# Pair-major order in 12 slots a pair, the MLP one batch behind, fp32 loads of batch 0, and deferred AV and output transposes

## The chip, the cores and the metric

The kernel runs on one core of a Trainium2 chip. The metric is the device time of one execution in microseconds. Each kernel was run several times. The kernel before takes 350.33 us (median of 4 runs, 350.21 to 351.83).

## The reference

Attention with a choice of key chunks, then a two-layer MLP with a softplus. There are 4 batches, 8 heads, 768 positions and 64 values a head; the MLP is 512 to 2048 to 512.

```python
k_min, k_max = k chunk-wise (24 chunks of 32 keys)
ub  = sum_d max(q*k_min, q*k_max)          # upper bound of each query for each chunk
top = the 6 best causal chunks of each query
p   = softmax(scale * q @ k.T, only the chosen chunks, causal)
x   = (p @ v) as [3072 tokens, 512]
out = softplus(x @ w_in) @ w_out           # float32
```

All inputs are float32 in memory; the kernel computes in bf16.

## The kernel before

Two heads make a pair: 4 pairs a batch, 16 in all. A pair is prepared (transposes of k and q, chunk maxima and minima, bound, choice of chunks, a mask row added to the score operands) and then has three blocks of 256 queries with 2, 4 and 6 score steps. A score step is two matmuls of up to 256 columns and one exp on ScalarE. An MLP block is 256 tokens; it needs the same block of all four pairs of its batch. It is cut into 8 `h` pieces (8 matmuls of 256 columns and an exp; after every second piece a log) and 8 `y` pieces (4 matmuls of 512 columns).

```python
def load(i):                                # all loads cast fp32 -> bf16 in flight, from GpSimd
    for h in range(2):
        nc.gpsimd.dma_start(out=k_sb[:, :, h, :], in_=k[b, 2*p+h]...)
        nc.gpsimd.dma_start(out=q_sb[:, :, h, :], in_=q[b, 2*p+h]...)
# ... load(0..2), load_v(0..2), then w_in (4 loads); w_out in the preparation of pair 1

steps = [(b*NP + p, blk) for b in range(B) for blk in range(NBLK) for p in range(NP)]  # block-major
for s_idx, st in enumerate(steps):
    # score_step(st); av_step of the step before; ot_step of the one before that;
    # preparation up to 6 steps ahead; the MLP paced by pump() at RATIO = 1.75
```

Each score step's diagonal block is masked by an `affine_select` on GpSimd; `av_step` multiplies by v into `o_ps` and divides into `o_sb`; `ot_step` transposes into `xT`, which the MLP reads. The framework's scheduler sets the order of the instructions on each engine; the order of the Python program is its input and is not always what stands in the queues.

The softmax here doesn't subtract the row's maximum and nothing guards it: scores larger than these inputs give would overflow.

## Time and profile before

| | before |
|---|---|
| median time | 350.33 us |
| TensorE busy | 281.8 us, 80% |
| first score exp | 28.7 us |
| first exp of the MLP ("MLP start") | 78.2 us |
| last score exp ends | 318.0 us |
| span minus MLP start | 272.3 us |

First, the page of the kernel before: busy time, the busy tenths in 40 slices of 8.76 us, and the chain that ended last.

```profile
PE 281.8 (80%) x2784; PEld 202.2 (58%) x2784; DVE 171.5 (49%) x580; ACT 218.1 (62%) x369; POOL 140.1 (40%) x274
...
PE   1003254389889989999999899999999999999994
...
POOL 8994877961682744350514443101112211000000
...
DMA  9999999990795864443703444000000000000111
...
PE 49%; POOL 16%; ACT 15%; DMA 7%; issue 7%; DVE 4%; POOLq 0%; ACTq 0%; DVEq 0%
```

TensorE (PE) is at most half busy in the first eight slices, in which GpSimd (POOL) is mostly full and the DMA engines are full; from slice nine on TensorE is nearly full. So an average of 80% hides two stages. The next view cuts the span at the MLP start and at the last score exp. Its columns are the busy time (and instructions) of PE, PEld, DVE, ACT and POOL, then the granted clock, the DMA share and GB/s.

```profile
0.00:78.20 78.20, 26.63 (x221) 19.32 (x222) 46.03 (x156) 16.47 (x27) 63.62 (x105) 1.00 1.43 124
78.20:318.00 239.80, 228.12 (x2387) 166.70 (x2386) 120.83 (x415) 188.70 (x326) 76.06 (x168) 1.00 0.32 39
318.00:350.50 32.50, 27.10 (x180) 16.16 (x177) 4.64 (x9) 12.95 (x18) 0.41 (x1) 0.98 0.11 41
```

TensorE works 26.6 of the first 78.2 us. By the timeline, only 15 of the 192 score exps are done by then. In the shared stretch it is busy 95%, but a busy TensorE is not one at its peak. The starts of its instructions give the better measure: an MLP piece takes 0.87 us, and a pair's whole attention about 5.3 us, 0.44 us a score step. Counted in the trace, with the cost of each kind of matmul that the prediction below lists, the shared stretch holds 177 score steps (192 - 15), about 161 MLP pieces and the preparations, AV products and transposes that fall into it: 214 us of work in 239.8 us. Part of the rest is in the list of waits of the kernel before from 78 us on (engine and line, whom it waited for: us in total, times, longest):

```profile
PEld L244 <- POOL pt L229: 10.4, 21, 1.2
PE o_ps L244 <- POOL pt L229: 6.6, 14, 1.1
```

The AV products (L244) wait for the diagonal select on GpSimd (L229). The two lines overlap, since PEld is the weight load of the same matmuls.

### The profile page before, as it was taken

The numbers are of one execution on the slowest core, as the hardware profiler recorded it, in microseconds if no ns is written. First come the engines' busy times: TensorE is split into PE (matmuls) and PEld (weight loads), VectorE is DVE, ScalarE is ACT, GpSimd is POOL, SyncE is SP. The second block draws the span as 40 slices with busy tenths as digits, with TensorE's granted clock in tenths as the row PEclk, the third lists the DMA queues.
The fourth block names the chain that finished last, engine by engine and source line by source line (L and its number), as shares of the span: only waits on it lengthen the run. The fifth ranks groups of instructions, "written<-read, shape, count | busy, mean of one in ns | idle before, by whom it ended". The sixth has DMA issues, their size and how long they took to land.

```text
span 350.5 us, 7076 instructions
## 1 busy us (share of the span) xinstructions
PE 281.8 (80%) x2784; PEld 202.2 (58%) x2784; DVE 171.5 (49%) x580; ACT 218.1 (62%) x369; POOL 140.1 (40%) x274
## 2 busy tenths in 40 slices
PE   1003254389889989999999899999999999999994
PEld 1002133268567656766776567767767777766651
DVE  3875285644773645674726456647165321212101
ACT  1102022259879749677987596879876878876640
POOL 8994877961682744350514443101112211000000
PEclk9999999999999999999999999999999999999999
DMA  9999999990795864443703444000000000000111
GB/s 67 80 145 189 136 192 129 109 66 1 49 86 37 77 46 54 52 30 49 75 33 36 41 55 52 2 32 32 30 32 4 33 30 32 30 2 32 46 46 60
DMA packets 81441, 20.38 MB, mean 58 GB/s; under 512 B 75776, under 2 KB 77824, under 8 KB 81408
## 3 DMA queue, kind: packets, MB, share of 16 engines
q0 software_dynamic: 77952, 13.64, 49.7%
q1 hardware_dynamic: 3456, 6.29, 4.8%
q8 instruction: 22, 0.36, 0.4%
q14 instruction: 11, 0.09, 0.1%
HBM read 27.26 MB, written 6.29 MB: 96 GB/s over the span
## 4 chain that ended last, share of the span: by engine, by line
PE 49%; POOL 16%; ACT 15%; DMA 7%; issue 7%; DVE 4%; POOLq 0%; ACTq 0%; DVEq 0%
PE hp L282 18%; PE y L297 15%; ACT pt L225 6%; PE o_ps L244 5%; ACT e_sb L284 4%; DMA w_out_sb<-in_moe_w_out_dram 4%; POOL k_sb L77 4%; PE s_ps L220 4%; POOL q_sb L79 4%; ACT g L286 3%; DMA w_in_sb<-in_moe_w_in_dram 3%; POOL pt L229 3%; PE s_ps L223 2%; PE mT L202 2%; PE kT L142 1%
## 5 line engine op out<-in xcount | busy, mean ns | idle before, releaser
L225 ACT ACTIVATE pt<-s_ps 128x512 bf16<-128x512 f32 (+1 forms) x192 | 99.6, 544 | 69.3 <-PE s_ps L223 68.2
L297 PE MATMUL y<-w_out_sb,g 128*128 128x512 bf16 x384 | 100.4, 379 | 1.6 <-DVE y_sb L302 1.6
L229 POOL TENSOR_SCALAR_AFFINE_SELECT pt<-pt 128x256 bf16<-128x256 bf16 x96 | 38.8, 409 | 127.2 <-ACT pt L225 126.1
L284 ACT ACTIVATE e_sb<-hp 128x512 f32<-128x512 f32 x96 | 57.0, 597 | 37.3 <-PE hp L282 36.5
L282 PEld LDWEIGHTS <-w_in_sb 128*128 128x128 bf16 x768 | 72.4, 99 | 13.4 <-issue 1.2
L282 PE MATMUL hp<-xT_221,w_in_sb 128*128 128x256 bf16 x192 | 53.1, 277 | 0.0
L282 PE MATMUL hp<-xT_222,w_in_sb 128*128 128x256 bf16 x192 | 52.7, 276 | 0.0
L282 PE MATMUL hp<-xT_223,w_in_sb 128*128 128x256 bf16 x192 | 52.3, 275 | 0.0
L282 PE MATMUL hp<-xT_224,w_in_sb 128*128 128x256 bf16 x192 | 51.6, 275 | 0.4
L286 ACT ACTIVATE g<-e_sb 128x1024 bf16<-128x1024 f32 x48 | 50.8, 1059 | 0.5
L244 PEld LDWEIGHTS <-pt 128*128 128x128 bf16 x672 | 33.5, 99 | 27.9 <-POOL pt L229 20.0
L297 PEld LDWEIGHTS <-g 128*128 128x128 bf16 x384 | 34.5, 97 | 25.6 <-issue 2.1
L249 DVE RECIPROCAL rec<-o_ps 128x4 f32<-128x4 f32 x48 | 8.5, 178 | 67.4 <-PE o_ps L244 67.4
L77 POOL DMA_DIRECT2D k_sb<-in_k_dram x32 | 27.3, 855 | 25.5 <-PE kT L142 21.3
L79 POOL DMA_DIRECT2D q_sb<-in_q_dram x32 | 27.3, 854 | 5.4 <-PE qT L156 3.5
L302 DVE COPY y_sb<-y 128x512 f32<-128x512 f32 x24 | 16.4, 684 | 26.3 <-PE y L297 26.3
L185 DVE TENSOR_TENSOR ub_sb<-ub,cmask 128x288 f32<-128x288 f32 x16 | 7.3, 454 | 27.3 <-PE ub L183 27.2
L251 DVE TENSOR_TENSOR o_sb<-o_ps,rec 128x256 bf16<-128x256 f32 x48 | 20.1, 418 | 1.1
L182 PEld LDWEIGHTS <-qpos 128*128 128x128 bf16 x96 | 7.3, 101 | 22.7 <-DVE qpos L171 17.0
L203 DVE COPY qa<-mT 32x768 bf16<-32x768 bf16 x16 | 8.8, 548 | 19.7 <-PE mT L202 19.7
L145 DVE TENSOR_REDUCE kx<-kT 128x24 bf16<-128x768 bf16 x16 | 15.2, 952 | 4.2 <-PE kT L142 4.0
L182 PE MATMUL ub<-bd_0_151,qpos 128*128 128x48 bf16 x48 | 4.4, 191 | 15.4 <-POOL bd_0_151 L151 14.2
(237 smaller groups left out, 461.7 us busy)
## 6 DMA issues: line engine op xcount, KB each, us to landing
out_dram<-y_sb SPq DMA_DIRECT2D x24, 256.0 KB, 2.0
k_sb<-in_k_dram POOLq DMA_DIRECT2D x32, 96.0 KB, 3.3
q_sb<-in_q_dram POOLq DMA_DIRECT2D x32, 96.0 KB, 3.5
w_in_sb<-in_moe_w_in_dram POOLq DMA_DIRECT2D x4, 512.0 KB, 8.9
w_out_sb<-in_moe_w_out_dram POOLq DMA_DIRECT2D x4, 512.0 KB, 10.3
v_98<-in_v_dram POOLq DMA_DIRECT2D x4, 96.0 KB, 3.8
v_99<-in_v_dram POOLq DMA_DIRECT2D x4, 96.0 KB, 3.3
v_100<-in_v_dram POOLq DMA_DIRECT2D x4, 96.0 KB, 3.5
```

Of the source, the lines that this page charges most:

```text
L77: nc.gpsimd.dma_start(out=k_sb[:, :, h, :], in_=k[b, 2 * p + h].rearrange("(t s) d -> s t d", s=128))
L79: nc.gpsimd.dma_start(out=q_sb[:, :, h, :], in_=q[b, 2 * p + h].rearrange("(t s) d -> s t d", s=128))
L145: nc.vector.tensor_reduce(kx[:, 0], kT3, axis=AX.X, op=ALU.max)
L225: nc.scalar.activation(pt[:, h, j:j + 2].rearrange("k j c -> k (j c)")[:, 0:n], s_ps[:, 0:n], ACT.Exp, scale=scale)
L229: nc.gpsimd.affine_select(out=diag, in_=diag, compare_op=ALU.is_ge, fill=0.0, base=0, channel_multiplier=-1, pattern=[[0, 2], [1, 128]])
L244: nc.tensor.matmul(o_ps[:, u, h], pt[:, h, j, c0:c0 + 128], v_sb[i % NV][:, j, h, :], start=(j == 0), stop=(j == t0 + u))
L251: nc.vector.tensor_tensor(o_sb, o_ps[:, :, :, 0:D], rec.to_broadcast([128, 2, 2, D]), op=ALU.mult)
L282: nc.tensor.matmul(hp[:, fi], w_in_sb[:, dt, ft * 128:(ft + 1) * 128], xT[dt][:, cs], start=(dt == 0), stop=(dt == KDM - 1))
L284: nc.scalar.activation(e_sb[:, f2 * 2:f2 * 2 + 2], hp, ACT.Exp)
L286: nc.scalar.activation(g[:, f4 * 4:(f4 + 1) * 4], e_sb, ACT.Ln, bias=1.0)
L297: nc.tensor.matmul(y, g[:, f, u * 128:(u + 1) * 128], w_out_sb[:, f, :], start=(f == 0), stop=(f == KFF - 1))
L302: nc.vector.tensor_copy(y_sb, y)
```

## The change

Its intent is to fill the idle start with attention work and to let TensorE wait less.

- Order: pair-major. A pair has 12 slots of one score step each; a slot also takes one deferred piece and one MLP piece, and slots 0, 1, 4 and 8 a piece of the next pair's preparation. The MLP runs about one batch behind. With the order came fewer buffers (k 8 to 4, v 12 to 5, q 8 to 4), one more for the MLP's `g`, and loads two pairs ahead instead of three.
- Loads: q and k of batch 0 come as fp32 from the SP queue (SyncE's DMA queue, HWDGE in the skill's terms) and are cast on ScalarE. The Trainium skill, "DMA: Bandwidth & Descriptors", section "SWDGE vs HWDGE vs iDMA", says that only GpSimd's DMAs can cast in flight; hence the fp32 buffers. For batch 0 some small copies also move from GpSimd to VectorE and from VectorE to ScalarE.
- Deferral: an AV product is due two slots after its scores, an output transpose two slots after its AV.

```diff
+    def load_f32(i):
+        for nm, x in (("k", k), ("q", q)):
+            xf = f_pool.tile([128, NQT, 2, D], F32, name="xf")      # 4 buffers
+            for h in range(2):
+                nc.sync.dma_start(out=xf[:, :, h, :], in_=x[b, 2 * p + h]...)
+            nc.scalar.copy(xb, xf)
-    load(1); load_v(1); load(2); load_v(2)
+    load_f32(1); load_v(1)
     for kt in range(KDM):                      # w_in: place unchanged
         nc.gpsimd.dma_start(out=w_in_sb[:, kt, :], in_=moe_w_in[...])
@@ prep_pair(i)
+        n = i + 2
+        load_f32(n) if n < NP else load_cast(n);  load_v(n)
@@ the order
+        later.append((clock[0] + 2, av_step(i, blk, pt)))        # and ot_step in the same way
+    PREP_AT = (0, 1, 4, 8)
+    for i in range(len(pairs)):
+        for blk in range(NBLK):
+            for _ in score_step(i, blk):
+                slot([nxt] if idx in PREP_AT else [])   # prep piece, one due piece, one MLP piece
...
```

More of the change, by code (lines that the diff above doesn't have):

```diff
@@ L1 @@
 import math
+from collections import deque
 from contextlib import ExitStack
@@ L43 @@
     NBLK = S // QB
-    NK = 8
-    NV = 12
+    NK = 4
+    NV = 5
     nc.scalar.preload_act_table_set("natural_log_exp_and_others")
+    PS = bass.MemoryType.PSUM
     singles = ctx.enter_context(tc.tile_pool(name="singles", bufs=1))
+    f_pool = ctx.enter_context(tc.tile_pool(name="f", bufs=4))
     io_pool = ctx.enter_context(tc.tile_pool(name="io", bufs=3))
-    qt_pool = ctx.enter_context(tc.tile_pool(name="qt", bufs=8))
+    qt_pool = ctx.enter_context(tc.tile_pool(name="qt", bufs=4))
     prep = ctx.enter_context(tc.tile_pool(name="prep", bufs=2))
@@ L54 @@
     st_pool = ctx.enter_context(tc.tile_pool(name="st", bufs=3))
-    g_pool = ctx.enter_context(tc.tile_pool(name="g", bufs=2))
+    g_pool = ctx.enter_context(tc.tile_pool(name="g", bufs=3))
     e_pool = ctx.enter_context(tc.tile_pool(name="e", bufs=3))
     mo_pool = ctx.enter_context(tc.tile_pool(name="mo", bufs=3))
-    PS = bass.MemoryType.PSUM
     ps_s = ctx.enter_context(tc.tile_pool(name="ps_s", bufs=2, space=PS))
@@ L67, with load_cast @@
     KB = [singles.tile([128, S], BF16, name=f"kb_{i}") for i in range(NK)]
+    w_in_sb = singles.tile([128, KDM, d_ff], BF16, name="w_in_sb")
+    w_out_sb = singles.tile([128, KFF, d_model], BF16, name="w_out_sb")
+    xT = [singles.tile([128, NTOK], BF16, name=f"xT_{p}") for p in range(NP)]
     pairs = [(b, p) for b in range(B) for p in range(NP)]
     loaded = {}
-    def load(i):
-        b, p = pairs[i]
-        q_sb = io_pool.tile([128, NQT, 2, D], BF16, name="q_sb")
-        k_sb = io_pool.tile([128, NQT, 2, D], BF16, name="k_sb")
-        for h in range(2):
-            nc.gpsimd.dma_start(out=k_sb[:, :, h, :],
-                                in_=k[b, 2 * p + h].rearrange("(t s) d -> s t d", s=128))
-            nc.gpsimd.dma_start(out=q_sb[:, :, h, :],
-                                in_=q[b, 2 * p + h].rearrange("(t s) d -> s t d", s=128))
-        loaded[i] = (q_sb, k_sb)
+    def load_f32(i):
+        for nm, x in (("k", k), ("q", q)):
+            xf = f_pool.tile([128, NQT, 2, D], F32, name="xf")
+            b, p = pairs[i]
+            for h in range(2):
+                nc.sync.dma_start(out=xf[:, :, h, :],
+                                  in_=x[b, 2 * p + h].rearrange("(t s) d -> s t d", s=128))
+            xb = io_pool.tile([128, NQT, 2, D], BF16, name=nm + "_sb")
+            nc.scalar.copy(xb, xf)
+            loaded[nm, i] = xb
+    def load_cast(i):
+        for nm, x in (("k", k), ("q", q)):
+            xb = io_pool.tile([128, NQT, 2, D], BF16, name=nm + "_sb")
+            b, p = pairs[i]
+            for h in range(2):
+                nc.gpsimd.dma_start(out=xb[:, :, h, :],
+                                    in_=x[b, 2 * p + h].rearrange("(t s) d -> s t d", s=128))
+            loaded[nm, i] = xb
     def load_v(i):
@@ L87, in load_v @@
                                 in_=v[b, 2 * p + h].rearrange("(t s) d -> s t d", s=128))
-    load(0)
-    load_v(0)
     ident = singles.tile([128, 128], BF16)
     make_identity(nc, ident)
+    load_f32(0)
+    load_v(0)
     cmask = singles.tile([128, NQT, NCH], F32, name="cmask")
@@ L114, with init_k @@
         nc.vector.memset(v_sb[i][:, :, :, D:D + 1], 1.0)
-    for i in range(NK):
+    def init_k(i):
         nc.vector.tensor_copy(KA[i][64:96, :], ohb)
@@ L118 @@
         nc.vector.tensor_copy(KB[i][32:64, :], ohb)
-    w_in_sb = singles.tile([128, KDM, d_ff], BF16, name="w_in_sb")
-    w_out_sb = singles.tile([128, KFF, d_model], BF16, name="w_out_sb")
-    load(1)
+    load_f32(1)
     load_v(1)
-    load(2)
-    load_v(2)
     for kt in range(KDM):
         nc.gpsimd.dma_start(out=w_in_sb[:, kt, :], in_=moe_w_in[kt * 128:(kt + 1) * 128, :])
-    xT = [singles.tile([128, NTOK], BF16, name=f"xT_{p}") for p in range(NP)]
-    QA = {}
-    QT = {}
+    QA, QT, owner = {}, {}, {}
     def prep_pair(i):
-        q_sb, k_sb = loaded.pop(i)
         ka, kb = KA[i % NK], KB[i % NK]
@@ L138, in prep_pair @@
         mraw = Mraw[i % 2]
+        early = i < NP
+        if i < NK:
+            init_k(i)
+        k_sb = loaded.pop(("k", i))
+        q_sb = loaded.pop(("q", i))
         kT = ps_t.tile([128, S], BF16, name="kT", tag="t")
@@ L148, in prep_pair @@
         nc.scalar.copy(kb[64:128, :], kT[64:128, :])
+        eng = nc.vector if early else nc.gpsimd
         for m, dst in enumerate((kmx, kmn)):
             for h in range(2):
-                nc.gpsimd.tensor_copy(dst[h * 64:(h + 1) * 64, h], kx[h * 64:(h + 1) * 64, m])
-        yield 0.35
+                eng.tensor_copy(dst[h * 64:(h + 1) * 64, h], kx[h * 64:(h + 1) * 64, m])
+        owner["k", i % NK] = i
+        yield
         qT = ps_t.tile([128, S], BF16, name="qT", tag="t")
@@ L156, in prep_pair @@
             nc.tensor.transpose(qT[:, t * 128:(t + 1) * 128], q_sb[:, t], ident)
-        if i + 3 < len(pairs):
-            load(i + 3)
-            load_v(i + 3)
+        n = i + 2
+        if n < len(pairs):
+            if n < NP:
+                load_f32(n)
+            else:
+                load_cast(n)
+            load_v(n)
+            owner["v", n % NV] = n
         if i == 1:
@@ L169, in prep_pair @@
         qneg = prep.tile([128, S], BF16, name="qneg")
-        nc.vector.tensor_copy(qt, qT)
+        if early:
+            nc.scalar.copy(qt, qT)
+        else:
+            nc.vector.tensor_copy(qt, qT)
         nc.vector.tensor_scalar_max(qpos, qt, 0.0)
@@ L174, in prep_pair @@
         QA[i], QT[i] = qa, qt
-        yield 0.35
-        yield 0.0
-        yield 0.0
+        yield
         ub = ps_t.tile([128, NQT, 2, NCH], F32, name="ub", tag="t")
@@ L194, in prep_pair @@
         nc.vector.tensor_copy(mraw[:, :, :, NCH:NCH + 1], m8[:, :, :, 0:1])
-        yield 0.35
-        yield 0.0
-        yield 0.0
-        yield 0.0
+        yield
         mT = ps_t.tile([64, S], BF16, name="mT", tag="t")
@@ L204, in prep_pair, with score_step @@
         nc.vector.tensor_copy(qt[32:64, :], mT[32:64, :])
-        yield 0.3
-    PT = {}
-    def score_step(st):
-        i, blk = st
+        yield
+    later = deque()
+    done = {}
+    clock = [0]
+    def score_step(i, blk):
+        assert owner["k", i % NK] == i
         t0 = 2 * blk
         pt = pt_pool.tile([128, 2, NQT, QB], BF16, name="pt")
-        PT[st] = pt
         for h in range(2):
@@ L226, in score_step, with av_step @@
                                      s_ps[:, 0:n], ACT.Exp, scale=scale)
-                yield 0.25
-            diag = pt[:, h, t0:t0 + 2, 0:128]
-            nc.gpsimd.affine_select(out=diag, in_=diag, compare_op=ALU.is_ge, fill=0.0,
-                                    base=0, channel_multiplier=-1,
-                                    pattern=[[0, 2], [1, 128]])
-    OS = {}
-    def av_step(st):
-        i, blk = st
+                if last:
+                    diag = pt[:, h, t0:t0 + 2, 0:128]
+                    nc.gpsimd.affine_select(out=diag, in_=diag, compare_op=ALU.is_ge, fill=0.0,
+                                            base=0, channel_multiplier=-1,
+                                            pattern=[[0, 2], [1, 128]])
+                yield
+        later.append((clock[0] + 2, av_step(i, blk, pt)))
+    def av_step(i, blk, pt):
         t0 = 2 * blk
-        pt = PT.pop(st)
         o_ps = ps_o.tile([128, 2, 2, D + 1], F32, name="o_ps")
@@ L246, in av_step @@
                                      start=(j == 0), stop=(j == t0 + u))
-            yield 0.1 * (t0 + u + 1)
+            if u == 0:
+                yield
         rec = st_pool.tile([128, 2, 2, 1], F32, name="rec")
@@ L252, in av_step, with ot_step @@
                                 rec.to_broadcast([128, 2, 2, D]), op=ALU.mult)
-        OS[st] = o_sb
-    def ot_step(st):
-        i, blk = st
+        later.append((clock[0] + 2, ot_step(i, blk, o_sb)))
+        yield
+    def ot_step(i, blk, o_sb):
         b, p = pairs[i]
-        o_sb = OS.pop(st)
         oT = ps_t.tile([128, QB], BF16, name="oT", tag="t")
@@ L264, in ot_step @@
         done[(b, blk)] = done.get((b, blk), 0) + 1
-        yield 0.12
-    done = {}
+        yield
     mlp_blocks = [(b, blk) for b in range(B) for blk in range(NBLK)]
+    G = {}
     def h_gen(n):
@@ L286, in h_gen @@
                     nc.scalar.activation(g[:, f4 * 4:(f4 + 1) * 4], e_sb, ACT.Ln, bias=1.0)
-                yield 0.87
-    G = {}
+                yield
     def y_gen(n):
@@ L304, in y_gen @@
                         nc.sync.dma_start(out=out[r0:r0 + 128, :], in_=y_sb)
-                    yield 0.87
+                    yield
     def mlp_stream():
@@ L309, in mlp_stream @@
         for n in range(len(mlp_blocks) + 1):
+            hg = iter(())
             if n < len(mlp_blocks):
                 while done.get(mlp_blocks[n], 0) < NP:
-                    yield None
+                    yield "wait"
                 hg = h_gen(n)
-            else:
-                hg = iter(())
             yg = y_gen(prev) if prev is not None else iter(())
-            for a in hg:
-                yield a
-                c = next(yg, None)
-                if c is not None:
-                    yield c
@@ L322, in mlp_stream @@
-            for c in yg:
-                yield c
+            for _ in hg:
+                yield
+                if next(yg, "end") != "end":
+                    yield
+            for _ in yg:
+                yield
             prev = n
     mlp = mlp_stream()
-    state = dict(attn=0.0, mlp=0.0)
-    ATT_TOTAL = 100.0
-    MLP_TOTAL = 167.0
-    RATIO = 1.75
-    LAG = 0.0
-    AHEAD = 6
-    def pump(cost):
-        state["attn"] += cost
-        while state["mlp"] < state["attn"] * RATIO - LAG:
-            c = next(mlp, "end")
-            if c is None or c == "end":
-                if c is None:
-                    state["mlp"] = max(state["mlp"], state["attn"] * RATIO - LAG - 2.0)
-                return
-            state["mlp"] += c
@@ L344, in chain @@
-    def chain(*gens):
-        for g_ in gens:
-            yield from g_
-    steps = []
-    for b in range(B):
-        for blk in range(NBLK):
-            for p in range(NP):
-                steps.append((b * NP + p, blk))
-    def drain(g_):
-        for c in g_:
-            pump(c)
-    side_done = []
-    def side_stream():
-        for i in range(len(pairs)):
-            yield from prep_pair(i)
-            side_done.append(i)
-    side = side_stream()
-    order = steps
-    for s_idx, st in enumerate(order):
-        while len(side_done) <= st[0]:
-            s = next(side, None)
-            if s is not None:
-                pump(s)
-        tail_gens = []
-        if s_idx >= 1:
-            tail_gens.append(av_step(order[s_idx - 1]))
-        if s_idx >= 2:
-            tail_gens.append(ot_step(order[s_idx - 2]))
-        tail = chain(*tail_gens)
-        ahead = order[min(s_idx + AHEAD, len(order) - 1)][0]
-        for c in score_step(st):
-            pump(c)
-            t_ = next(tail, None)
-            if t_ is not None:
-                pump(t_)
-            if len(side_done) <= min(ahead + 1, len(pairs) - 1):
-                s = next(side, None)
-                if s is not None:
-                    pump(s)
-        for t_ in tail:
-            pump(t_)
@@ L390, with slot @@
-    drain(av_step(order[-1]))
-    drain(ot_step(order[-2]))
-    drain(ot_step(order[-1]))
-    for c in mlp:
+    def slot(piece_gens=()):
+        for g_ in piece_gens:
+            next(g_, None)
+        if later and later[0][0] <= clock[0]:
+            g_ = later[0][1]
+            if next(g_, "end") == "end":
+                later.popleft()
+                if later and later[0][0] <= clock[0]:
+                    next(later[0][1], None)
+        next(mlp, None)
+        clock[0] += 1
@@ L394 @@
+    PREP_AT = (0, 1, 4, 8)
+    for _ in prep_pair(0):
+        pass
+    for i in range(len(pairs)):
+        nxt = prep_pair(i + 1) if i + 1 < len(pairs) else iter(())
+        idx = 0
+        for blk in range(NBLK):
+            for _ in score_step(i, blk):
+                slot([nxt] if idx in PREP_AT else [])
+                idx += 1
+        for _ in nxt:
+            pass
+    while later:
+        slot()
+    for _ in mlp:
         pass
```

## The prediction

> **What bounds the kernel now.** TensorE is busy 80% of the 350.5 us (page, part 1), but unevenly. The 40 slices and the table by window show two regimes. From 0 to about 77 us TensorE is busy under 40%; the last chain of waits there runs through GpSimd issuing casting loads (k_sb and q_sb, about 0.85 us each) and through waits for the w_in and w_out DMAs (11.9 and 13.2 us pieces). From about 80 us on TensorE is 90-100% busy and the chain is hp and y matmuls. The MLP's first pieces stand at about 77 us in the chain; it then needs 270 us.
>
> **Costs read from the timeline (start to start).** One MLP piece takes 0.87 us (8 hp matmuls at 0.109, or 4 y matmuls at 0.215). Per pair: kT and qT 0.34 each, ub 0.30, mT 0.46, scores 2.3, AV 42 x 0.03 = 1.26, oT 3 x 0.11: about 5.3 us, 0.44 per score slot. Sum: 192 x 0.87 + 16 x 5.3 = 252 us that TensorE must spend. A slot plus a piece is 1.31 us of TensorE work; before needs about 1.42 (windows 140 to 260: about 84 slots and 85 pieces). ScalarE needs about 1.05 us per such slot, so TensorE stays the bound there.
>
> **What changes.** Nothing leaves TensorE. (1) Pair-major order needs all four pairs of a batch nearly finished before its MLP starts: by the slot rules at slot 43; it pauses at slots 83 to 91, and some 50 pieces are left after the last slot (50 x 0.87 = 43 us, TensorE alone, well packed). (2) Before 77 us the kernel now does 43 attention slots, against about 10 before: that fills the idle start. (3) Batch 0's q and k leave the casting queue: GpSimd issues 2 loads a pair instead of 6 (saves about 3.4 us a pair) and no longer copies bd early. The Trainium skill, "DMA: Bandwidth & Descriptors", section on SWDGE vs HWDGE, says that a cast in flight is possible only from GpSimd, hence the fp32 buffers and ScalarE casts (estimate 0.8 us each from the 0.79 us copies). The same page says that all issuers share 16 DMA engines, so bytes and 256-byte descriptors still queue there; the trace has no such HWDGE load to show their rate. (4) AV and oT deferred two slots: removes most TensorE waits for the diagonal select (about 20 us of waits over the span, about 10 in the first 80 us).
>
> **Sum.** First slot: ScalarE's in-order queue makes pair 0's qt copy wait for casts of pairs 1 and 2, which compete with w_in: landing about 20-22 us, plus a 6 us selection chain: 28 us. Attention-only slots are bound by VectorE (about 10.6 us of work a pair) and ScalarE (about 9): 43 slots at 0.95 = 41 us, MLP start at 69 us. Then 141 shared slots at 1.36 = 192, 8 slots alone 7, 51 pieces 44, last y copy and store 3. Total 315 us.
>
> **Prediction: 315 us, range 299 to 337.** Faster by over 2%: 0.91; within 2%: 0.07; slower by over 2%: 0.02.
>
> **What the profile would show.** First score exp at 22-34 us; first hp matmul at 60-78 us; in the shared stretch 16.3 us per pair with TensorE over 95% busy; a pure MLP tail of 38-46 us; waits of o_ps for the select nearly gone; ScalarE waits for DMA xf in the first 25 us.
>
> **What would make it wrong.** HWDGE loads with 256-byte descriptors far slower than 0.8 descriptors per ns (seen for GpSimd's loads), or starved by w_in: each pair's delay adds directly before the MLP start. Shared slots no better than 1.42: +8 us. Attention-only slots chain-bound at 1.2 us: +11 us.

## The result, and the profile after

The changed kernel takes 322.9 us (median of 4 runs, 322.04 to 323.86). The ratio to the kernel before is 0.9209 (95% interval 0.9173 to 0.9245).

The page after, same lines without DMA:

```profile
PE 278.0 (86%) x2784; PEld 203.4 (63%) x2784; DVE 167.9 (52%) x573; ACT 225.0 (70%) x381; POOL 123.9 (38%) x242
...
PE   1213788698999999899999999999999999999984
...
POOL 8401688846444545558191919131212111000000
...
PE 78%; ACT 7%; SPq 4%; DMA 4%; DVE 3%; issue 2%; POOL 1%; ACTq 0%; POOLq 0%
```

The chain is now 78% TensorE instead of 49%, with GpSimd down from 16% to 1%. The stretches of the kernel after, cut at the same events:

```profile
0.00:79.80 79.80, 44.26 (x421) 32.08 (x422) 48.15 (x182) 41.77 (x71) 45.18 (x77) 0.89 1.15 132
79.80:270.50 190.70, 188.32 (x2055) 142.74 (x2055) 113.44 (x380) 158.56 (x279) 78.36 (x164) 1.00 0.46 48
270.50:322.00 51.50, 45.41 (x311) 28.61 (x309) 6.34 (x11) 24.65 (x33) 0.41 (x1) 0.99 0.11 42
```

This is the main reading. The MLP does not start earlier: 79.8 us against 78.2. But by then 47 score exps are done instead of 15, and what follows takes 242.2 us (322.0 - 79.8) instead of 272.3. Counted in the two traces as above, the TensorE work before the MLP start is 22.9 us after and 12.3 before, so about 10.6 us moved into the start. (The 32 steps at 0.44 would make 14, but the 0.44 includes the preparation, which was about equally far in both kernels: the k and q of five pairs were transposed.) The shared stretch now holds 145 score steps and about 140 pieces, 185 us of work in 190.7, so about 6 us are lost where before lost about 26. The sum, 10.6 + 20, is about the 30 us that the part after the MLP start became shorter. The select's waits after 80 us are nearly gone:

```profile
PEld L260 <- POOL pt L247: 0.3, 1, 0.3
PEld L277 <- DVE o_sb L268: 0.3, 1, 0.3
```

(L260 is the AV product and L277 the output transpose of the kernel after.)

Why does the MLP not start earlier, with fewer loads on GpSimd? The timeline of the SP queue after (start, us, what):

```profile
0.81 1.01 SPq L82 DMA_DIRECT2D xf<-in_k_dram  x2
1.88 1.21 SPq L82 DMA_DIRECT2D xf<-in_q_dram  x2
3.13 2.92 SPq L82 DMA_DIRECT2D xf<-in_k_dram  x2
6.10 2.35 SPq L82 DMA_DIRECT2D xf<-in_q_dram  x2
8.57 11.29 SPq L82 DMA_DIRECT2D xf<-in_k_dram  x2
```

and of ScalarE, with GpSimd's w_in line between:

```profile
7.80 2.18 POOL L138 DMA_DIRECT2D w_in_sb<-in_moe_w_in_dram  x4
...
24.19 0.83 ACT L85 CAST q_sb<-xf 128x768 bf16<-128x768 f32 x1 [10.23 <-DMA xf<-in_q_dram]
25.05 0.79 ACT L160 COPY kb_110<-kT 64x768 bf16<-64x768 bf16 x1
...
29.37 0.83 ACT L85 CAST q_sb<-xf 128x768 bf16<-128x768 f32 x1 [0.85 <-DMA xf<-in_q_dram]
30.23 0.87 ACT L243 ACTIVATE pt<-s_ps 128x384 bf16<-128x384 f32 x2
```

Pair 1's q was issued at 6.1 us. w_in was issued from 7.8 us on, and the q landed only at 24.2 us; the SP queue's next two issues took 11.29 us (2.83 us for the same two in e7 below, where no weight is in flight). ScalarE works in order: pair 0's last k copy (25.05) stood behind the cast of pair 1's q, and the first score exp, whose matmul began at 26.5 us, stood behind the cast of pair 2's q (29.37) and came at 30.2 us.

The packets that the packed trace records show the crowding itself. From 12 to 20 us, beside w_in, the SP queue's packets of 256 bytes start at 53 per us, about one for each of w_in's 48 packets of 4096 bytes per us. From 27 to 31 us, alone, they start at 822 per us.

A second thing stands in the timeline of TensorE in the attention-only stretch of the kernel after:

```profile
39.04 0.42 PE L238 MATMUL s_ps<-qa,ka_106 96*128 96x256 bf16 x1
39.26 0.31 PE L241 MATMUL s_ps<-qa,ka_106 96*128 96x128 bf16 x1
...
92.83 0.27 PE L238 MATMUL s_ps<-qa,ka_106 96*128 96x256 bf16 x1
92.94 0.27 PE L241 MATMUL s_ps<-qa,ka_106 96*128 96x256 bf16 x1
```

The matmul of 256 columns keeps TensorE 0.22 us at 39 us and 0.11 us at 92 us. The Trainium skill, "TensorE: Matmul & The Clock Gate", Part 1, says that the array runs at half its clock by default and that sustained activity releases it; the factor of two agrees. The page's clock column shows 1.00 at 39 us all the same, because it has no record before 48.4 us (in the kernel before, none before 79.6 us, so the 1.00 of its first stretch is no measurement either). Between 64 and 72 us it records 0.50.

### The profile page after: what moved, and what is told of

It reads as the page before. It is cut to its first block, busy times and chain, and to the rows that moved or that the text cites. A ratio compares the mean times of both kernels' runs of the same rounds, so it can differ in the third digit from the quotient of the medians.

```text
span 322.0 us, 7075 instructions
## 1 busy us (share of the span) xinstructions
PE 278.0 (86%) x2784; PEld 203.4 (63%) x2784; DVE 167.9 (52%) x573; ACT 225.0 (70%) x381; POOL 123.9 (38%) x242
## 3 DMA queue, kind: packets, MB, share of 16 engines
q1 hardware_dynamic: 16000, 9.44, 10.6%
## 4 chain that ended last, share of the span: by engine, by line
PE 78%; ACT 7%; SPq 4%; DMA 4%; DVE 3%; issue 2%; POOL 1%; ACTq 0%; POOLq 0%
PE y L311 26%; PE hp L298 25%; PE o_ps L260 7%; PE s_ps L238 7%; PE s_ps L241 5%; SPq L82 4%; DMA xf<-in_q_dram 4%; ACT pt L243 3%; PE mT L219 3%; PE oT L277 2%; PE kT L154 2%; PE qT L170 1%; ACT e_sb L300 1%; DVE y_sb L316 1%; PE ub L203 1%
## 5 line engine op out<-in xcount | busy, mean ns | idle before, releaser
L243 ACT ACTIVATE pt<-s_ps 128x384 bf16<-128x384 f32 (+1 forms) x192 | 101.3, 548 | 30.0 <-PE s_ps L241 27.9
L311 PE MATMUL y<-w_out_sb,g 128*128 128x512 bf16 x384 | 98.2, 379 | 1.6 <-DVE y_sb L316 1.6
L247 POOL TENSOR_SCALAR_AFFINE_SELECT pt<-pt 128x256 bf16<-128x256 bf16 x96 | 40.1, 426 | 135.7 <-ACT pt L243 134.5
L298 PEld LDWEIGHTS <-w_in_sb 128*128 128x128 bf16 x768 | 70.7, 98 | 12.9 <-issue 1.2
L260 PEld LDWEIGHTS <-pt 128*128 128x128 bf16 x672 | 32.5, 103 | 4.4 <-issue 1.6
L93 POOL DMA_DIRECT2D k_sb<-in_k_dram x24 | 20.1, 839 | 7.1 <-PE kT L154 6.4
L93 POOL DMA_DIRECT2D q_sb<-in_q_dram x24 | 20.6, 861 | 0.8 <-issue 0.6
L154 PE MATMUL kT<-ident,k_sb 128*128 128x128 bf16 x96 | 9.3, 242 | 13.4 <-ACT kb_110 L160 7.1
L266 DVE RECIPROCAL rec<-o_ps 128x4 f32<-128x4 f32 x48 | 8.4, 176 | 22.9 <-PE o_ps L260 22.6
L277 PE MATMUL oT<-ident,o_sb 128*128 128x128 bf16 x96 | 14.2, 232 | 2.0 <-DVE o_sb L268 2.0
L154 PEld LDWEIGHTS <-k_sb 128*128 128x128 bf16 x96 | 7.0, 109 | 13.7 <-issue 7.3
```

Source lines behind the costliest of these rows:

```text
L93: nc.gpsimd.dma_start(out=xb[:, :, h, :], in_=x[b, 2 * p + h].rearrange("(t s) d -> s t d", s=128))
L154: nc.tensor.transpose(kT[:, t * 128:(t + 1) * 128], k_sb[:, t], ident)
L243: nc.scalar.activation(pt[:, h, j:j + 2].rearrange("k j c -> k (j c)")[:, 0:n], s_ps[:, 0:n], ACT.Exp, scale=scale)
L247: nc.gpsimd.affine_select(out=diag, in_=diag, compare_op=ALU.is_ge, fill=0.0, base=0, channel_multiplier=-1, pattern=[[0, 2], [1, 128]])
L260: nc.tensor.matmul(o_ps[:, u, h], pt[:, h, j, c0:c0 + 128], v_sb[i % NV][:, j, h, :], start=(j == 0), stop=(j == t0 + u))
L277: nc.tensor.transpose(oT[:, u * 128:(u + 1) * 128], o_sb[:, u], ident)
```

## The experiments

My theory has two parts. O: the order pays by moving score steps into the start, and the deferral by removing waits; the fp32 loads pay little. S: the MLP start is late because w_in starves the SP loads. The rivals are named in the expectations. This table collects all runs, in us; the events are from the profiled run, the median from the timed runs.

| run | first score exp | MLP start | span | span minus MLP start | median | ratio to before |
|---|---|---|---|---|---|---|
| before | 28.7 | 78.2 | 350.5 | 272.3 | 350.3 | |
| after | 30.2 | 79.8 | 322.0 | 242.2 | 322.9 | 0.9209 |
| e1_w_in_late | 25.7 | 75.0 | 317.2 | 242.2 | 319.8 | 0.9108 |
| e2_cast_loads | 19.0 | 80.9 | 322.9 | 242.0 | 324.7 | 0.9239 |
| e3_no_defer | 30.2 | 81.8 | 334.0 | 252.2 | 335.4 | 0.9542 |
| e4_warm | 29.9 | 79.6 | 322.4 | 242.8 | 323.8 | 0.9216 |
| e5_before_f32 | 43.9 | 78.9 | 351.1 | 272.2 | 353.1 | 1.0063 |
| e6_gate2 | 23.9 | 76.7 | 318.5 | 241.8 | 320.6 | 0.9136 |
| e7_gate3 | 23.7 | 78.8 | 320.8 | 242.0 | 322.0 | 0.9179 |
| e8_gate3_warm2 | 22.4 | 77.0 | 319.9 | 242.9 | 322.8 | 0.9196 |
| e9_w_out_late | 29.5 | 76.3 | 318.8 | 242.5 | 320.1 | 0.9113 |
| e10_gate2_w_out_late | 22.8 | 68.6 | 310.4 | 241.8 | 313.6 | 0.8926 |
| e11_gate2_w_out_late_warm2 | 23.8 | 70.9 | 313.7 | 242.8 | 314.6 | 0.8944 |
| e12_order_only | 20.4 | 81.0 | 331.9 | 250.9 | 333.6 | 0.9502 |

The column "span minus MLP start" is the key: it has only three levels. It is 272 with the old order, 251 to 252 with the new order without deferral, and 242 to 243 with both. No load or weight experiment changes it. So the time is the MLP start plus a constant set by order and deferral, and the two questions can be treated apart.

### What each part of the change is worth: e2, e3, e5, e12

e2 takes the fp32 loads back:

```diff
-    load_f32(0) ... load_f32(1) ... load_f32(n)
+    load_cast(0) ... load_cast(1) ... load_cast(n)
```

> The changed kernel with q and k of batch 0 loaded as before, by casting DMAs on GpSimd, and no casts on ScalarE; all else as changed. Theory O (the order is what pays): the loads of pairs 0 and 1 now stand before w_in in one queue, so nothing is starved, ScalarE is relieved of 8 casts of 0.83 us, GpSimd issues 16 more loads of 0.85 us; the two effects about cancel: 318-328 us. Rival L (the loads are what pays): GpSimd's issue time and its waits for the queue come back, as in the kernel before, and the MLP starts 10 us or more later: 333 us or more.

Measured: 324.7 us, ratio 0.9239 (0.9203 to 0.9274); the interval overlaps that of the changed kernel. O holds. The first score even comes 11 us earlier (19.0 us), with no cast before it in ScalarE's queue, but the MLP starts at 80.9 us: ScalarE is busy only 1.65 of the 10 us from 30 to 40 us, while GpSimd is busy 9.33.

e5 is the kernel before with the fp32 loads alone:

```diff
 def load(i):
+        if i < NP:
+            # k and q as fp32 on nc.sync into xf (3 buffers), then nc.scalar.copy
```

> The kernel before with one part of the change alone: q and k of batch 0 loaded as fp32 by the SP queue and cast on ScalarE (three fp32 buffers); its block-major order and its MLP pacing stay. Theory O (the order is what pays): the loads alone bring little; w_in still starves the SP loads of pairs 1 and 2, so the MLP's first exp stays within 5 us of 78 us and the time is 343-352 us. Rival L: freeing GpSimd of 16 loads pays by itself: MLP start before 68 us and the time under 340 us.

Measured: 353.1 us, ratio 1.0063 (1.0043 to 1.0083), which is 0.6% slower. The expected range had 352 as its end, so it was missed by 1 us; L is refuted. The first score is 15 us later (43.9 us), yet the MLP start stays at 78.9.

e3 takes the deferral away:

```diff
-        later.append((clock[0] + 2, av_step(i, blk, pt)))
+        later.append((clock[0], av_step(i, blk, pt)))       # the same for ot_step
```

> The changed kernel with the AV products and the output transposes handed over as soon as they exist (+0 slots instead of +2). Theory D (deferral pays): TensorE waits again for the diagonal select on GpSimd and for o_sb, o_ps waits of 10 us or more in total come back, and a shared slot goes from 1.32 to about 1.40 us: 332-337 us. Rival: the order of TensorE's instructions is set mostly by what is ready when the program is scheduled, and pair-major order alone leaves the select enough time: 322-326 us.

Measured: 335.4 us, ratio 0.9542 (0.9506 to 0.9579). D holds in size, but of the two waits that it names it is mainly the one for o_sb that returns. The waits of e3 from 82 us on:

```profile
PEld L277 <- DVE o_sb L268: 9.5, 21, 0.9
PEld L260 <- POOL pt L247: 3.0, 9, 0.8
```

The output transpose waits for the division on VectorE (9.5 us), the AV product for the select only 3.0 us. The pair-major order alone already spares most of the select's wait (10.4 us before); the deferral spares the one for o_sb. The part after the MLP start is 10.0 us longer than with deferral (252.2 - 242.2), and the MLP starts 2 us later. By the count of work used above, the shared stretch of e3 loses about 16 us, against 26 before and 6 after: the order and the deferral each spare about 10 us of waits.

e12 has the order alone: the edits of e2 and e3 together.

> The changed kernel without two of its three parts: casting loads for batch 0, and no deferral; what is left is the pair-major order in 12 slots with one MLP piece a slot (and the copies of the first batch on VectorE and ScalarE). If the parts add: 323 + 12.5 (no deferral) + 1.8 (casting loads) = 337 us, so 335-339 us. If the loads matter more without deferral, or less: outside 334-341 us.

Measured: 333.6 us, ratio 0.9502 (0.9479 to 0.9525). The expected sum was 337 and the time fell just outside even the wider 334 to 341, so the parts do not add exactly: without deferral the casting loads are about 2 us better than the fp32 loads (335.4 in e3), with deferral about 2 us worse (324.7 against 322.9). These two differences are of the size of the intervals, and I draw nothing from them but that the loads are worth about zero beside weights that start early; with the weights held back, as in e10 below, casting loads were not tried. From the order, with its buffers and small copies, comes about 17 us (350.3 to 333.6), from the deferral about 9 (333.6 to 324.7) or, with the fp32 loads, 12.5 (335.4 to 322.9).

### Why the MLP does not start earlier: e1, e6, e7, e9, e10

e1 moves w_in in the program, from before the first preparation to the preparation of pair 1.

```diff
-    for kt in range(KDM): nc.gpsimd.dma_start(out=w_in_sb[:, kt, :], ...)    # before prep_pair(0)
+        if i == 1:                                                           # in prep_pair(i)
+            for kt in range(KDM): nc.gpsimd.dma_start(out=w_in_sb[:, kt, :], ...)
```

> The changed kernel with one edit: the four w_in loads are issued on GpSimd in the preparation of pair 1, after pair 3's loads, instead of before the first preparation. Theory S (starvation): the q of pair 1, issued at 6.1 us and landed at 24.2 us in the changed kernel, waits behind w_in's large packets on the shared DMA engines, and ScalarE's in-order queue passes that on to the first score. Then pair 1's q lands before 13 us, the first score exp moves from 30.2 to about 20-22 us, the MLP's first exp from 79.8 to about 70-72 us, and the time falls from 323 to 312-315 us. Rival A (absorbed): the stretch up to the MLP is bound by the attention chain itself, or w_in now starves pair 2 and 3 instead; then the first exp moves, but the MLP start moves by less than 4 us and the time stays within 320-324 us.

Measured: 319.8 us, ratio 0.9108 (0.9065 to 0.915); the time fell by about 3 us, not by 8 to 11. The casts of e1 on ScalarE and w_in's issue on GpSimd:

```profile
11.11 1.16 POOL L178 DMA_DIRECT2D w_in_sb<-in_moe_w_in_dram  x2
...
13.22 0.83 ACT L85 CAST q_sb<-xf 128x768 bf16<-128x768 f32 x1 [1.18 <-DMA xf<-in_q_dram]
...
24.87 0.83 ACT L85 CAST q_sb<-xf 128x768 bf16<-128x768 f32 x1 [6.11 <-DMA xf<-in_q_dram]
```

Pair 1's q now lands at 13.2 us instead of 24.2: starvation by w_in is shown. The Trainium skill, "DMA: Bandwidth & Descriptors", section "Issuing engines are not separate DMA queues", says that loads of all issuers run on the same 16 DMA engines and interleave; these 11 us agree. But nothing on GpSimd made w_in wait, so the scheduler let it go at 11.1 us, and now pair 2's q was late (24.9 us), which rival A had named as a possibility. The MLP start moved by 4.8 us, between what S and A expected. An issue that only stands later in the program is not later on the chip.

e6 and e7 hold the weights back by data. A one-row copy on GpSimd from a q tile into the weight's tile must finish before the load may overwrite it:

```diff
+        if i == 0:      # e6; e7: i == 1 and pair 3's q
+            nc.gpsimd.tensor_copy(w_in_sb[0:1, :, 0:1], loaded["q", 2][0:1, 0, 0, 0:KDM].unsqueeze(2))
+            # then the four w_in loads
         if i == 1:
+            # the same kind of copy from pair 3's q before the four w_out loads
```

> The changed kernel with w_in's loads held back by data: a one-row copy from pair 2's q tile into w_in's tile stands before them on GpSimd (w_out the same with pair 3's q), so that the weights cannot be issued earlier; e1 moved them only in the program, and GpSimd still issued w_in at about 12 us. Theory S (starvation by w_in): now the q of pairs 1 and 2 land by about 13 and 18 us; first score exp at about 19-21 us, MLP start at about 69-72 us, time 311-315 us. Rival A (the attention chain absorbs it): first exp earlier, MLP start not before 74 us, time 317-321 us. Rival W: w_in itself becomes late: TensorE waits on w_in at the MLP start.

> As the run before, with w_in held back until pair 3's q is cast, so no weight competes with any batch-0 load on the SP queue. Theory S: at most 2 us better than the hold at pair 2, because pair 3 is needed only from slot 24 on: 310-315 us. Rival W: w_in and w_out together (about 25 us of transfer in the traces) now reach to about 50 us and hold back the casting loads of pair 4 and the diagonal selects that stand behind them on GpSimd: 316 us or more.

Measured: 320.6 us (ratio 0.9136, 0.9114 to 0.9158) and 322.0 us (0.9179, 0.9145 to 0.9214). The first score came at 23.9 and 23.7 us, 6 us earlier than after, but the MLP started only 3.1 and 1.0 us earlier. S's number for the time was missed in both. The numbers of e6 are those of its rival A (MLP start 76.7 us, time 320.6), and e7 came out as its rival W said. The chain of e6 in the window 28 to 55 us has

```profile
32.30 16.43 DMA w_out_sb<-in_moe_w_out_dram
```

and GpSimd's timeline

```profile
47.06 0.82 POOL L93 DMA_DIRECT2D q_sb<-in_q_dram  x1 [2.29 <-DMA w_out_sb<-in_moe_w_out_dram]
49.54 0.83 POOL L93 DMA_DIRECT2D q_sb<-in_q_dram  x1 [1.65 <-DMA w_out_sb<-in_moe_w_out_dram]
...
51.18 0.43 POOL L251 TENSOR_SCALAR_AFFINE_SELECT pt<-pt 128x256 bf16<-128x256 bf16 x1
```

GpSimd's issues of pair 4's q and k wait up to 2.29 us each for w_out's transfers, and a diagonal select stands behind them in the same queue. The operands in the packed trace say what they wait for: GpSimd's loads use eight semaphores in turn, and an issue waits until the load before it on the same semaphore has landed (the one at 49.54 waits for semaphore 103, that of w_out's last load). So the program waits here, by semaphores that the framework set. The trace doesn't show e6's A, an attention chain that absorbs the gain, nor e6's W, a late w_in; it shows w_out filling GpSimd's queue. In e7 the same piece is 16.09 us long.

e9 and e10 test that. Both move w_out to the preparation of pair 3, behind a copy from pair 4's q; e10 also holds w_in back as e6 does.

```diff
-        if i == 1:
+        if i == 3:
+            for c4 in range(4): nc.gpsimd.tensor_copy(w_out_sb[0:1, c4*4, 0:1], loaded["q", 4][0:1, 0, 0, 0:1])
             for c4 in range(4): nc.gpsimd.dma_start(out=w_out_sb[:, c4*4:(c4+1)*4, :], ...)
```

> The changed kernel with only w_out moved: it is loaded in the preparation of pair 3 behind a one-element copy from pair 4's q, instead of in the preparation of pair 1. In the two hold-back runs the first score came 6 us earlier, but the MLP start only 1 to 3 us: w_out then filled GpSimd's queue (a 16 us piece of the chain), and diagonal selects and pair 4's loads stood behind it. Theory G (after the first score, GpSimd's in-order queue behind w_out limits the stretch): MLP start at about 74-77 us, time 317-320 us. Rival V (the stretch is bound by the attention work of TensorE at half clock, VectorE and ScalarE): MLP start within 1.5 us of 79.8 us, time 321-324 us.

> w_in held back until pair 2's q is cast, and w_out until pair 4's q is there. Theory G: the 6 us gained at the first score (30.2 to about 23.8) now reach the MLP start: 70-74 us, time 313-317 us. Rival V: attention chain bound; MLP start 75 us or later, time 318-322 us.

Measured: e9 320.1 us (ratio 0.9113, 0.909 to 0.9137), 0.1 us outside G's range, with the MLP start inside it (76.3 us); e10 313.6 us (0.8926, 0.8895 to 0.8957), as expected of G, with an MLP start 1.4 us earlier than G's 70 to 74. The stretches of e10:

```profile
0.00:68.60 68.60, 39.57 (x421) 28.68 (x422) 49.48 (x182) 41.59 (x70) 46.38 (x82) 0.90 1.38 154
68.60:259.30 190.70, 188.30 (x2055) 142.75 (x2056) 113.67 (x380) 158.63 (x279) 77.97 (x164) 1.00 0.46 48
```

The shared stretch is 190.70 us, the same as after to the digit; the whole gain is the MLP start, 68.6 us instead of 79.8. (The profiled run after was the slowest of its four and that of e10 the fastest of its four; by the medians the gain is 9.3 us.) Moving w_in alone (e1), w_out alone (e9), or both with w_out still too soon (e6) brings the MLP start forward by 3 to 5 us each; both held back far enough bring 11.2. While one is in the way, moving the other lets the work run into the next wait. e10 beats both kernels. It computes the same result, and it is 2.8 points of ratio below the changed kernel (0.8926 against 0.9209), with intervals far apart.

### Does the half clock bind the attention-only stretch: e4, e8, e11

These add matmuls of 256 columns to the first 43 slots, into a PSUM tile that nobody reads (4 in e4, 2 in e8 and e11):

```diff
+    def warm():
+        wt = ps_h.tile([128, 2, QB], F32, name="hp")
+        for r in range(4):
+            nc.tensor.matmul(wt[:, r % 2], ident, KB[0][:, 0:QB], start=True, stop=True)
```

> The changed kernel with four extra 256-column matmuls a slot in the first 43 slots, into a PSUM tile that nobody reads (the result is unchanged). Theory C (clock): in the attention-only stretch of the changed kernel the TensorE records a granted clock of 0.5 for much of 52 to 79 us, and matmuls of 256 columns start 0.217 us apart instead of 0.109; if that limits the stretch, keeping the clock at 1.0 moves the MLP start from 79.8 to about 72-75 us and the time to 315-319 us, although 37 us of work at full clock is half added. Rival: the stretch is bound by VectorE and ScalarE chains; then the clock goes to 1.0, start-to-start falls to 0.109, and the MLP start and the time do not fall (322-330 us).

> The run before plus two extra 256-column matmuls a slot in the first 43 slots (result unchanged). With four (e4) the granted clock rose to 1.0 from 40 to 70 us but the MLP start did not move, because at full clock 4 x 0.109 us is as much as the half clock costs (0.44 us a slot). With two, a slot needs 0.66 us of TensorE at full clock against 0.89 at half clock. Theory C (the half clock limits the stretch): MLP start 3-8 us earlier than in the run before, time 2-8 us less. Rival V (VectorE and ScalarE bind the stretch, about 10.6 and 9 us of work a pair): no change or worse, within 2 us of the run before.

> The run before plus two extra 256-column matmuls a slot in the first 43 slots (result unchanged): the test of the half clock without w_out in the way. Theory C: with the clock at 1.0 the stretch from the first score to the MLP start shrinks by 3-6 us. Rival V: it shrinks by less than 1.5 us or grows.

Measured: e4 323.8 us (ratio 0.9216, 0.9179 to 0.9253), e8 322.8 (0.9196, 0.9155 to 0.9237), e11 314.6 (0.8944, 0.8907 to 0.8981). The stretch from the first score to the MLP start is 49.8 us in e4 (49.6 after), 54.6 in e8 (55.1 in e7) and 47.1 in e11 (45.9 in e10). In e4 the clock did rise:

```profile
50.00:70.00 20.00, 17.93 (x246) 14.49 (x243) 17.30 (x65) 12.68 (x23) 14.44 (x24) 1.00 1.05 68
```

But four matmuls of 0.109 us are 0.44 us a slot, as much as the full clock spares, so the total of e4 cannot tell the theories apart. In e8 and e11 two a slot did not hold the clock up to the end (in e11 it is 1.00 from 21 to 41.5 us, then 0.58 from 40 to 50 us and 0.74 from 50 to 60 us). And the extra matmuls did not stay in their slots: the scheduler bunched them before the last score steps. In e4:

```profile
72.15 2.98 PE L343 MATMUL hp<-kb,ident 128*128 128x256 bf16 x16
```

All the extra matmuls together are 27.6% of e4's chain from the first score to the MLP start. Until that block e4 was ahead: its 42nd score exp starts 41.7 us after the first, against 44.5 us in the kernel after, but the next five take 11.1 us against 2.7. In e8 (48.3 against 48.7 us in e7) and e11 (40.7 against 40.3 us in e10) there is no such lead. By the letter of the expectations the rival V is favoured, since no stretch got clearly shorter; but the tests carried a load of their own, and e4's lead, seen in one profiled run, is a hint of C. Whether the half clock binds this stretch stays open.

## Why the prediction was right or wrong, point by point

The predicted time was 315 us with a range of 299 to 337; measured 322.9, inside the range; it is faster by more than 2%, which had been given a chance of 0.91. The range is wide, 5 to 7% to each side, and two errors in the sum partly cancelled, as the points show.

- Two stages before, and TensorE's 252 us of work as the base: right. The work per step and piece, summed, explains the shared stretch after to within 6 us of 190.7.
- "Shared slots at 1.36": about right. With the 8 slots alone the prediction has 199 us for 149 slots, 1.34 each; after takes 190.7 / 145 = 1.32 us, 15.8 us a pair against the 16.3 written, with TensorE busy 188.3 of 190.7.
- Deferral removes most waits for the select: right in effect (9 to 10 us after the MLP start: e12 against e2, e3 against after), but the mechanism was half right. The order spares most of the select's wait; the deferral mainly spares the wait for o_sb, which the prediction did not name.
- "(3) Batch 0's q and k leave the casting queue", listed as a saving of GpSimd's time: it is worth about nothing (e2, e5).
- w_in starves the SP loads, through ScalarE's in-order queue: right in effect, half right in detail. It was not pair 0's qt copy that waited (it ran at 12.5 us, and the selection chain was done by 20.0), but its last k copy, for pair 1's q (24.2 us), and the first exp, for pair 2's q (29.4 us). That "28 us" for the first slot is near the 26.5 of the first score matmul and the 30.2 of its exp is partly luck.
- "First hp matmul at 60-78 us": missed. It stands at 38.6 us. An h piece sums over the four pairs, and the scheduler put the part of a pair into TensorE's queue early; the first part that needs pair 3 runs at 79.0 us.
- "43 slots at 0.95 = 41 us, MLP start at 69 us": this is the mis-sized term. It measured 47 score exps in 49.6 us (79.8 - 30.2), 1.06 us each. The 43 follow from the Python slots, but 47 score steps stand in TensorE's queue before the first hp matmul that needs pair 3: 4 x 0.95 = 3.8 us. The rate was too fast by about 0.105 x 47 = 4.9 us. With the 2.2 us of the first exp this makes the 10.8 us by which the MLP start was missed; the part after it was 242.2 us against 246 predicted (315 - 69), which happened to give about 4 us back.
- What sets the rate of that stretch is shown in part: with both weights out of the way it falls to 45.9 us (e10). The half clock is open.
- A pure MLP tail of 38 to 46 us: about 47 us (270.5 to the last y copy at about 318).

## What to carry to other kernels

Find the event after which variants of one order take the same time (here the first MLP exp); then a start experiment is read from that event and an order experiment from the rest, and neither hides the other. A large weight load on the same DMA engines was best held back here by a data dependency until the first inputs had landed, and both weights had to be moved: moving one only uncovered the next. Handing over a product two steps late paid 9 to 12 us here.

## What the Trainium skill lacked or had wrong

- "DMA: Bandwidth & Descriptors", section "Issuing engines are not separate DMA queues", calls the sequencer's time to issue a DMA usually small relative to the DMA itself. Beside w_in the SP queue needed 11.29 us for two issues that took 2.83 us in e7, with no weight in flight.
- The same page has no rate measured on trn2 for HWDGE loads with 256-byte rows. In the kernel after, the SP queue's 256-byte packets start at 822 per us alone (27 to 31 us), about 590 per us beside v's loads (2 to 9 us) and 53 per us beside w_in (12 to 20 us).
- "TensorE: Matmul & The Clock Gate" is right about the default half clock (0.22 against 0.11 us for 256 columns), but no page says that the profile's clock column reads 1.00 until its first record; here that was at 48.4 us.
